# The opening of a DeltaNet and maxout kernel: one root for the inverse squares, a transposition in halves, the fourth query products later, two PSUM tiles exchanged

## The chip, the cores and the metric

The kernel runs on one core of one Trainium2 chip. The metric is the time of one execution in microseconds (us) on the device. Before the change three runs gave 506.69, 509.49 and 509.79 us; the median is 509.49 us. Beside these there is one profiled execution, and all positions and durations below are from it.

## The reference

Two stages follow each other. The first is a recurrence over 768 time steps for 4 batches with 8 heads each, with a state of 48x48 per head. The second is a maxout layer over the 3072 tokens of width 384.

```python
k_n = k / (np.linalg.norm(k, axis=-1, keepdims=True) + 1e-06)
for t in range(S):
    y[:, :, t] = np.einsum('bhd,bhde->bhe', q[:, :, t], state)
    v_old = np.einsum('bhde,bhd->bhe', state, kt)
    state = state + bt[:, :, :, None] * np.einsum('bhd,bhe->bhde', kt, vt - v_old)
...
h = np.maximum(np.maximum(x @ w1, x @ w2), x @ w3)
return h @ w_out
```

## The kernel before

**Tiling.** The recurrence is cut into 12 chunks of 64 steps. Inside a chunk the updates are a unit triangular system; its inverse is built from the Gram matrix of the keys. Two chunks make a group, and there are 6 groups (`GROUPS`). A group's 512 tokens are one tile of the maxout layer. `ffn(m)` is a generator: it issues the matrix products of one tile and yields after each hidden product (`p_h`), and the loop at the end of the kernel puts pieces of the next group's recurrence between the yields. So TensorE (PE) always has the dense products of `ffn` and, between them, the small ones of the recurrence.

**Order.** The whole kernel is issued under a schedule written by hand: each engine executes its instructions in the order in which the program lists them, and waits for others by semaphores. A late instruction therefore holds up everything behind it on its engine.

**The opening.** Before the first `p_h` the first group has to go through the recurrence with little else to do. The stages, with the lines of the profile:

- Keys are loaded, transposed on PE (`turn`, L338; ACT copies the result out, L344), and multiplied to Gram matrices (`gram`, L415). The part for keys gives `at` (L432), the part for queries (index 1) gives `pt` (L426), which is masked later (L399).
- `solve(0)` takes the 32x32 blocks of the first two chunks, with one block per partition, in `x_bl`. The diagonal holds the squares of the key norms. `norm` (L270 to L275) takes the root on ACT and improves it with one Newton step in five small VectorE (DVE) instructions; a reciprocal, a square and a product with beta follow (L532 to L534), and the scaling of `x_bl` (L547). Then 15 steps of two DVE instructions (L561, L565) build `y_bl`, the inverses of the blocks, in halves of 16.
- `y_bl` is transposed back (L573) and `placed` (L505) copies four pieces of it into `ut`, for chunk 0 at once and for chunk 1 over the following stages.
- `halves_t(0)` transposes `ut` (L645, L647) into two tiles `t`. `halves_z` (`p_e`, L685), `halves_u` (`p_f`, L696), `turn_t1` (L630, L632), `join_z` (`p_z`, L713) and `join_u` (`p_j`, L726) join the halves to 32 and then to 64: two products each, copied or negated out of PSUM by ACT (L688, L700, L717, L728) and, for a part, by DVE.
- `scale` (L296, on GpSimd, here POOL) multiplies the values by the key norms, `new` (`p_u`, L771) applies the inverse, `to_y` (`p_y`, L813) multiplies by the masked `pt`, `to_x` (`p_x`, L832) transposes the result into `xt` (L839), and the first `p_h` (L1224) can start. `solve(1)` then runs on DVE between the pieces of `ffn(0)`; its `y_p` lies in PSUM.

**The weights.** They arrive as 64-bit floats, read as pairs of 32-bit words. `weights()` is a generator (`conv`): each call lets ACT convert one piece (L247 to L249) and then finishes the piece *before* it by a shift on DVE (L259) and an addition on POOL (L263, in `joined`). The pieces come in the order of use: piece 0 is for the first `p_h`, piece 1 for the second, and so on. Four calls are made before `ffn(0)`; in the loop the call of step `i` finishes piece `i`+3 (`CONVERTED`). The tile `w_bits` has five buffers and `mant` two, so a later conversion also delays the fetch into its buffer.

**The tables.** `FIRST` says what the loop of `ffn(0)` issues behind the hidden product number `i`+1: `e1` is `halves_z(1)`, `f1` `halves_u(1)`, `k1` and `q1` the products with the state (`p_k`, `p_q`, L743), `z1`, `j1`, `u1`, `y1`, `s1`, `x1` the other stages of chunk 1, `M2` the mask of `pts[2]`, `T4` the transposition of query unit 4, `P4` the query part of Gram unit 4, and `S1` one step of `solve(1)`.

**The end.** The last group uses products of 7 instead of 8 blocks. `crossed_hidden` makes the hidden values in 6 units of 8 small products each (L1163); `bank(n)` gives the PSUM tile of product `n`. Tiles of `ps_ffn` (two buffers) serve products 6 and 7, tiles of `banks` (six buffers) the others. Products 3 and 4 are copied out by ACT (L1193, L1197), 6 and 7 are added by DVE (L1169). `outputs` (L985) then takes its two PSUM tiles from `ps_ffn`.

Of the kernel before, what the change touches and what calls it, by code (L numbers as in the profile page):

```python
# [14 lines left out]
ALU = mybir.AluOpType  # L15
# [8 lines left out]
def kernel(  # L24
# [243 lines left out]
    def norm(out, ksum, root, t):  # L268
# [8 lines left out]
        )  # L277

    def small(name, *shape):
        one = name[-1] == "0" or name[-2:] == "bl" or name == "warm"  # L280
        return work.tile([128, *shape], FP32, name=name, bufs=2 - one)
# [215 lines left out]

    def placed(cc, i, copy=nc.vector.tensor_copy, xs_of=slice(0, 2 * H)):
# [6 lines left out]
        copy(to[:, xs_of], of[:, xs_of])  # L505

    def solve(m):
# [13 lines left out]
        bl = small("bl", BL)  # L521
        norm(bl, diagonal(x), small("root_bl", BL), small("nt_bl", BL))
        if m == 1:
            y = ps_two("y_p").rearrange("p b (j i) -> p (b j) i", i=BL)
            nc.scalar.copy(y, zero.to_broadcast(y.shape))
        if m:
            norms_of(m, bl)
            nc.vector.reciprocal(bl, bl)
        else:
            bl_0.append(bl)  # L530
            bl = small("inv_bl", BL)
            nc.vector.reciprocal(bl, bl_0[0])  # L532
        nc.vector.tensor_tensor(out=bl, in0=bl, in1=bl, op=ALU.mult)
        nc.vector.tensor_tensor(out=bl, in0=bl, in1=beta_bl[:, m] if m else beta_0, op=ALU.mult)  # L534
        if m > 2:
# [35 lines left out]
        if m == 0:  # L571
            back = in_rows(xs[0])
            nc.vector.transpose(out=back, in_=y.rearrange("p c i -> p i c"))  # L573
            yield
            for i in range(4):
                if i % 2:
                    n = H * (i == 3)
                    if n:
                        placed(0, i, nc.vector.tensor_copy, slice(0, n))
                    placed(0, i, nc.scalar.copy, slice(n, 2 * H))  # L580
                else:
                    placed(0, i, nc.vector.tensor_copy)
            return
# [54 lines left out]

    def halves_t(c, parts=(0, 1)):
        if c not in fine:  # L640
            fine[c] = [square("t") for g in range(2)]
        src = [ut[c % NU][:, g].rearrange("p h x -> p (h x)") for g in range(2)]
        dst = [t.rearrange("p h x -> p (h x)") for t in fine[c]]
        if 0 in parts:
            nc.vector.transpose(out=dst[0], in_=src[0])  # L645
        for bb in range(2) if 1 in parts else ():
            nc.vector.transpose(out=dst[1][rows(1 - bb)], in_=src[1][rows(bb)])  # L647

# [27 lines left out]
    def halves_z(c):  # L676
        if c > 1:
            halves_t(c)
        at = [ats[2 * c + g] for g in range(2)]
        second = ut[c % NU].rearrange("p g h (f two x) -> p g h f two x", two=2, x=HB)  # L680
        for hs, p_v, copy in heads_of(c, "p_e", BL):
            for i, h in enumerate(hs):
                for bb, g in TILES:
                    r = rows(bb)
                    nc.tensor.matmul(  # L685
                        p_v[rows(bb ^ g), g, i], at[g][r, h], second[r, g, h, :, 1]
                    )
            copy(zs[c % NU][:, :, span(hs)], p_v)  # L688

# [435 lines left out]
    def crossed_hidden(m, hs):  # L1125
# [24 lines left out]
        for unit in range(2 * PAIRS):  # L1150
# [24 lines left out]
            def bank(n):  # L1175
                if n > 5:
                    return ps_ffn([128, TOK], "p_e")[:, 0:256]
                return banks.tile([128, TOK], FP32, name="p_c", tag="one", bufs=6)[
                    :, 0:256
                ]  # L1180
# [151 lines left out]
    load_q(3, (nc.gpsimd, nc.gpsimd))  # L1332
    load_beta()
    keys(6)
    gram(0, (1,), None, later=True)
# [16 lines left out]
    placed(1, 1, nc.gpsimd.tensor_copy)  # L1352
    blocks(1, nc.gpsimd)
    for _ in range(2):
# [4 lines left out]
    masked(pts[0], by_par(pts[0]))  # L1359
    placed(1, 2)  # L1360
    join_u(0)
# [193 lines left out]
```

## Time and profile before

| | us |
|---|---|
| runs | 506.69, 509.49, 509.79; median 509.49 |
| profiled execution | 507.8 |
| its span, first to last instruction | 506.1 |
| PE busy in the span | 484.4 |
| DVE, ACT, POOL busy | 362.5, 168.7, 186.4 |
| start of the first `p_h` | 45.39 |

The chain of waits goes back from the last instruction to what released it, step by step. The windows give each engine's busy time and the granted TensorE clock (PEclk) in a stretch. The timeline lists instructions in order of time: start, duration, engine, line, what is written and read, and in brackets how long the engine had been idle and who ended that.

### The profile page before, as it was taken

What the parts mean: (1) busy time and instruction counts of PE and PEld (TensorE: products, weight loads), DVE (VectorE), ACT (ScalarE), POOL (GpSimd) and SP (SyncE); (2) the same over time, 40 slices, a digit from 0 to 9 for tenths busy, and PEclk for the clock granted to TensorE, in tenths of its full rate; (3) what the DMA queues carried; (4) which work ended last, traced back from release to release, by engine and by line L of the source; (5) the groups of instructions that cost most, each with busy time, mean ns of one, the idle gap of its engine ahead of it and who ended that gap; (6) DMA issues with size and microseconds to landing.
All of it is one profiled execution on the core that took longest, in us unless ns stands there. A gap on an engine that the chain in (4) does not pass through costs nothing.

```text
span 506.1 us, 18677 instructions
## 1 busy us (share of the span) xinstructions
PE 484.4 (96%) x8064; PEld 338.0 (67%) x8064; DVE 362.5 (72%) x835; ACT 168.7 (33%) x320; POOL 186.4 (37%) x311
## 2 busy tenths in 40 slices
PE   7678899999999999999999999999999999999996
PEld 6567688756565555565555565555797457998795
DVE  5888989868996431799562999565998865467843
ACT  4576854884422142210153200252211042113210
POOL 6424582783491925870495870601000020000000
PEclk9855999999999999999999999999999999999999
DMA  8937979783055925443585552834224321330002
GB/s 111 205 53 207 201 177 147 183 220 91 2 141 128 191 57 122 121 118 99 120 157 124 138 139 62 168 56 93 63 61 88 62 66 25 89 80 0 0 17 47
DMA packets 109122, 53.50 MB, mean 106 GB/s; under 512 B 92209, under 2 KB 102865, under 8 KB 109041
## 3 DMA queue, kind: packets, MB, share of 16 engines
q1 hardware_dynamic: 97280, 31.78, 31.2%
q0 software_dynamic: 9216, 19.85, 15.6%
q8 instruction: 63, 1.03, 0.9%
q10 hardware_dynamic: 2544, 0.69, 0.7%
q14 instruction: 19, 0.15, 0.1%
HBM read 39.17 MB, written 13.11 MB: 103 GB/s over the span
## 4 chain that ended last, share of the span: by engine, by line
PE 82%; DVE 6%; DMA 5%; ACT 2%; issue 1%; SPq 1%; POOL 1%; ACTq 0%; DVEq 0%; POOLq 0%
PE p_h L1224 31%; PE p_o L985 13%; PE p_o L1262 12%; PE p_c L1163 4%; PE p_g L415 3%; PE p_u L771 3%; PE p_m L905 2%; PE p_k L743 2%; PE p_y L813 2%; PE p_q L743 2%; PE p_s L794 2%; PE p_j L726 2%; DMA x_bl<-at_d 1%; DMA qall<-in_q_dram 1%; PE p_e L1163 1%
## 5 line engine op out<-in xcount | busy, mean ns | idle before, releaser
L1224 PE MATMUL p_h<-xt,w_sb 128*128 128x512 f32 (+1 forms) x450 | 187.5, 559 | 1.3 <-issue 0.7
L1224 PEld LDWEIGHTS p_h<-xt,w_sb 128*128 128x128 f32 x450 | 82.5, 193 | 70.0 <-issue 62.4
L1238 DVE TENSOR_TENSOR h<-h,p_h 128x512 f32<-128x512 f32 (+1 forms) x42 | 25.4, 606 | 47.2 <-PE p_h L1224 45.7
L565 DVE TENSOR_TENSOR y_bl<-y_bl,tmp 128x31 f32<-128x31 f32 (+20 forms) x139 | 50.3, 362 | 4.8
L561 DVE TENSOR_TENSOR tmp<-x_bl,y_bl 128x31 f32<-128x31 f32 (+20 forms) x139 | 48.7, 350 | 3.9
L1262 PE MATMUL p_o<-wo_sb,h 128*128 128x384 f32 x144 | 48.9, 490 | 0.0
L373 POOL DMA_DIRECT2D turned<-in_q_dram x72 | 39.1, 551 | 4.3 <-POOL turned L368 2.9
L1262 PEld LDWEIGHTS p_o<-wo_sb,h 128*128 128x128 f32 x144 | 26.8, 190 | 17.2
L1234 ACT ACTIVATE h<-p_h 128x512 f32<-128x512 f32 x24 | 14.3, 597 | 69.3 <-PE p_h L1224 69.2
L263 POOL TENSOR_TENSOR w_sb<-mant,up 128x384 int32<-128x384 int32 x18 | 18.8, 1046 | 37.7 <-DVE mant L259 34.7
L415 PEld LDWEIGHTS p_g<-kqt 48*64 48x64 f32 x1216 | 24.9, 143 | 9.3 <-issue 6.7
L415 PE MATMUL p_g<-kqt 48*64 48x64 f32 (+1 forms) x1216 | 28.1, 243 | 0.9 <-ACT kqt L344 0.8
L1268 ACT COPY o_sb<-p_o 128x384 f32<-128x384 f32 x12 | 5.7, 479 | 62.6 <-PE p_o L1262 56.5
L399 DVE TENSOR_TENSOR pt<-p_g,mask 128x512 f32<-128x512 f32 x20 | 13.8, 689 | 16.2 <-PE p_g L415 16.0
L801 DVE TENSOR_TENSOR st<-st,p_s 48x768 f32<-48x768 f32 (+1 forms) x18 | 17.1, 949 | 11.1 <-PE p_s L794 10.8
L598 POOL DMA_DIRECT2D ut<-y_d x4 | 2.6, 651 | 60.4 <-DMA y_d<-y_bl 60.4
L148 POOL DMA_DIRECT2D v_t<-in_v_dram x14 | 11.5, 829 | 36.0 <-PE p_u L771 36.0
L368 POOL MEMSET turned<- 128x96 f32 x18 | 3.3, 191 | 49.6 <-DVE kqt L389 49.6
L771 PEld LDWEIGHTS p_u<-v_t,ut 64*64 64x64 f32 x768 | 13.7, 144 | 7.9 <-issue 5.9
L432 ACT COPY at<-p_g 128x512 f32<-128x512 f32 x22 | 12.7, 583 | 18.6 <-DVE pt L399 16.1
L373 POOL DMA_DIRECT2D turned<-in_k_dram x32 | 17.4, 553 | 1.2 <-POOL turned L368 1.2
L129 POOL DMA_DIRECT2D kpad<-in_k_dram x24 | 16.4, 691 | 3.0 <-PE p_s L794 3.0
(241 smaller groups left out, 909.2 us busy)
## 6 DMA issues: line engine op xcount, KB each, us to landing
w_bits<-in_moe_w_dram SPq DMA_DIRECT2D x9, 384.0 KB, 5.8
w_bits<-in_moe_w_dram POOLq DMA_DIRECT2D x9, 384.0 KB, 6.3
turned<-in_q_dram POOLq DMA_DIRECT2D x72, 48.0 KB, 2.8
out_dram<-o_sb SPq DMA_DIRECT2D x36, 96.0 KB, 2.3
y_x<-y SPq DMA_DIRECT2D x32, 96.0 KB, 2.2
qall<-y_x SPq DMA_DIRECT2D x32, 96.0 KB, 2.6
v_t<-in_v_dram POOLq DMA_DIRECT2D x14, 192.0 KB, 5.0
at_d<-at SPq DMA_DIRECT2D x72, 32.0 KB, 2.5
```

The lines of the kernel that those rows point to most:

```text
L263: nc.gpsimd.tensor_tensor(out=dst.bitcast(I32), in0=mant_v.bitcast(I32), in1=up_v, op=ALU.add)
L373: (queue, nc.gpsimd)[i].dma_start(out=t[p0 : p0 + 32, bb, at : at + NP * 2 * D].rearrange("p (j x) -> p j x", j=NP), in_=(k, q)[i][2 * bb ...
L415: nc.tensor.matmul(p_g[rows(bb ^ (g * i)), par, c0 : c0 + C * (1 + whole)], kq[:, 0], kq if whole else kq[:, i],)
L561: nc.vector.tensor_tensor(out=t_v, in0=row.to_broadcast(t_v.shape), in1=column.to_broadcast(t_v.shape), op=ALU.mult,)
L565: nc.vector.tensor_tensor(out=rest, in0=rest, in1=t_v, op=ALU.subtract)
L743: nc.tensor.matmul(p_b[rows(bb), par, c0 : c0 + D], kqt[g][dims(par), j, bb ^ g, i], st[dims(par), bb ^ g, g, j],)
L771: nc.tensor.matmul(p_v[rows(bb ^ g), g, i], ut[c % NU][rows(bb), g, h], rhs[rows(bb), g, h],)
L985: nc.tensor.matmul(to[:, g], a[j][:, 128 * g : 128 * (g + 1)], b[j], start=(start and g == j == 0), stop=(stop and g == 1 and j == len(a) ...
L1163: nc.tensor.matmul(to, w[stays], moves, start=(n == 0), stop=(n == len(terms) - 1))
L1224: nc.tensor.matmul(p_h, w_sb[i][:, t, f * 128 : (f + 1) * 128], xt[:, t, lo : lo + w], start=(t == 0), stop=(t == KT - 1),)
L1238: nc.vector.tensor_tensor(out=h, in0=h, in1=p_h, op=ALU.max)
L1262: nc.tensor.matmul(p_o, stays, moves, start=(n == 0), stop=(n == len(terms) - 1))
```

## The change

It has six parts. (1) `inverse_squares` makes 1/(norm+eps)² directly: ACT takes the root of 4·eps²·ksum, one DVE instruction adds eps² and ksum, one takes the reciprocal. The norms themselves, still needed for the values, are made by `first_roots`: a root on ACT and four small instructions on POOL, behind the issue of the beta loads. (2) The solution is transposed by columns in two halves (`turn_back`), the second half first, and `placed` copies by column halves, first the columns that `p_e` reads. (3) The tiles `t` are no longer transposed from `ut`: POOL sets them to zero (`zero_halves`), one DVE transposition turns the first half of the solution (`turn_half`), and eight small copies place its blocks, for chunk 0 on DVE and ACT, for chunk 1 on DVE. (4) The query transposition of unit 3 moves behind `to_x(0)`, its products into step 3 of the loop (`P3` in place of `M3`). (5) One call of `conv` before the solution is left out, and step 6 of the loop gets one. The four pieces of `placed(1, ...)`, one of which POOL copied, move to the stages around `to_y(0)` and all go to DVE; `solve(1)` starts behind `to_x(0)` and not ahead of it. ACT alone copies `p_e` out. (6) In `bank`, products 3 and 4 use `ps_ffn`, 6 and 7 use `banks`.

```diff
+    def inverse_squares(out, square_of, ksum):
+        nc.scalar.activation(out=square_of, in_=ksum, func=Sqrt, scale=4.0 * EPS * EPS)
...
+    def first_roots():
...
+        nc.scalar.sqrt(out, square_of)
+        mult(out=t, in0=out, in1=out, op=ALU.mult)
+        mult(out=t, in0=t, in1=inverse, op=ALU.mult)
+        nc.gpsimd.tensor_scalar(
+            out=t, in0=t, scalar1=-0.5, scalar2=1.5, op0=ALU.mult, op1=ALU.add
+        )
+        mult(out=out, in0=out, in1=t, op=ALU.mult)
...
+    def turn_back(s):
+        cols = slice(HB * s, HB * (s + 1))
+        nc.vector.transpose(
+            out=in_rows(xs[0])[:, cols], in_=ys[0].rearrange("p c i -> p i c")[:, cols]
+        )
...
+    def turn_half():
+        nc.vector.transpose(
+            out=first_half().rearrange("p c x -> p (c x)"),
+            in_=ys[0][:, 0:HB].rearrange("p c i -> p (c i)"),
+        )
+    def halves_t(c, engines):
+        for n, engine in enumerate(engines):
+            f, bb, g = n // 4, n // 2 % 2, n % 2
...
+            copy(
+                fine[c][g][block(bb ^ g, f), :, BL * f : BL * f + HB],
+                first_half()[block(bb, f), :, x0 : x0 + H].rearrange("p c h -> p h c"),
+            )
...
-                if n > 5:
+                if n in (3, 4):
                     return ps_ffn([128, TOK], "p_e")[:, 0:256]
...
     load_beta()
+    first_roots()
+    zero_halves(0)
+    zero_halves(1)
     keys(6)
...
-    turn(3, (1,))
-    some(conv, 1)
     gram(2, (1,), None, later=True)
-    gram(3, (1,), None, later=True)
-    some(solving, HB + 1)
-    halves_t(0)
+    some(solving, HB)
+    turn_back(1)
+    for i in range(4):
+        placed(0, i, A.copy if i % 2 else V.tensor_copy, high)
+    turn_half()
+    halves_t(0, (V, A, V, A, V, A, V, V))
     halves_z(0)
+    turn_back(0)
+    for i in range(4):
+        placed(0, i, V.tensor_copy, low)
     first_norms()
     some(conv, 1)
-    placed(1, 0)
     scale(0, nrm_0[:, 0])
-    placed(1, 1, nc.gpsimd.tensor_copy)
...
     load_v(1, nc.gpsimd)
+    placed(1, 0)
+    placed(1, 2)
+    to_y(0)
     placed(1, 3)
-    to_y(0)
-    halves_t(1)
+    placed(1, 1)
+    halves_t(1, (V, V, V, V, V, V, V, V))
     solving = solve(1)
+    to_x(0)
+    turn(3, (1,))
     some(solving, 1)
-    to_x(0)
     some(conv, 1)
...
-        3: "j1 S1 q1 M3 S1 S1", 4: "u1 T4", 5: "y1", 6: "s1 T5", 7: "x1 T6",
+        3: "j1 S1 q1 P3 S1 S1", 4: "u1 T4", 5: "y1", 6: "s1 T5", 7: "x1 T6",
...
-    CONVERTED = {*range(6), *range(11, 25)}
+    CONVERTED = {*range(7), *range(11, 25)}
```

More of the change, by code (lines that the diff above doesn't have):

```diff
@@ L277, in norm @@
         )
+    EPS = 1e-6
+    def inverse_squares(out, square_of, ksum):
+        nc.scalar.activation(
+            out=square_of, in_=ksum, func=mybir.ActivationFunctionType.Sqrt,
+            scale=4.0 * EPS * EPS,
+        )
+        nc.vector.scalar_tensor_tensor(
+            out=square_of, in0=square_of, scalar=EPS * EPS, in1=ksum,
+            op0=ALU.add, op1=ALU.add,
+        )
+        nc.vector.reciprocal(out, square_of)
+    def first_roots():
+        out, square_of, inverse = bl_0
+        t, mult = small("root_bl", BL), nc.gpsimd.tensor_tensor
+        nc.scalar.sqrt(out, square_of)
[5 more added lines that the diff above has]
+        mult(out=out, in0=out, in1=t, op=ALU.mult)
     def small(name, *shape):
@@ L495, in blocks, with placed @@
         )
-    def placed(cc, i, copy=nc.vector.tensor_copy, xs_of=slice(0, 2 * H)):
+    ys = []
+    def turn_back(s):
[3 more added lines that the diff above has]
+        )
+    def placed(cc, i, copy=nc.vector.tensor_copy, cols=slice(0, BL)):
         bb, half = divmod(i, 2)
@@ L504, in placed @@
         of = in_rows(xs[0])[r, :, 16 * cc : 16 * (cc + 1)].rearrange("p i x -> p x i")
-        copy(to[:, xs_of], of[:, xs_of])
+        copy(to[:, :, cols], of[:, :, cols])
     def solve(m):
@@ L521, in solve @@
         bl = small("bl", BL)
[L522 to L525, printed above, removed]
         if m:
+            norm(bl, diagonal(x), small("root_bl", BL), small("nt_bl", BL))
+            if m == 1:
+                y = ps_two("y_p").rearrange("p b (j i) -> p (b j) i", i=BL)
+                nc.scalar.copy(y, zero.to_broadcast(y.shape))
             norms_of(m, bl)
             nc.vector.reciprocal(bl, bl)
+            nc.vector.tensor_tensor(out=bl, in0=bl, in1=bl, op=ALU.mult)
         else:
[L530 to L534, printed above, removed]
+            bl_0.extend((bl, small("square_bl", BL), small("inv_bl", BL)))
+            bl = small("nt_bl", BL)
+            inverse_squares(bl_0[2], bl_0[1], diagonal(x))
+        nc.vector.tensor_tensor(
+            out=bl, in0=bl if m else bl_0[2], in1=beta_bl[:, m] if m else beta_0,
+            op=ALU.mult,
+        )
         if m > 2:
@@ L571, in solve @@
         if m == 0:
[L572 to L582, printed above, removed]
+            ys.append(y)
             return
@@ L637, with zero_halves, first_half @@
     fine = {}
[L639 to L647, printed above, removed]
+    def zero_halves(c):
+        fine[c] = [square("t") for g in range(2)]
+        zeros(*fine[c])
+    def first_half():
+        return in_wo(1)[:, 0, 0 : HB * BL].rearrange("p (c x) -> p c x", x=BL)
+    def turn_half():
+        nc.vector.transpose(
+            out=first_half().rearrange("p c x -> p (c x)"),
+            in_=ys[0][:, 0:HB].rearrange("p c i -> p (c i)"),
+        )
+    def halves_t(c, engines):
+        for n, engine in enumerate(engines):
+            f, bb, g = n // 4, n // 2 % 2, n % 2
+            x0 = 16 * c + 8 * g
+            copy = nc.scalar.copy if engine is nc.scalar else engine.tensor_copy
+            copy(
+                fine[c][g][block(bb ^ g, f), :, BL * f : BL * f + HB],
+                first_half()[block(bb, f), :, x0 : x0 + H].rearrange("p c h -> p h c"),
+            )
     def heads_of(c, name, w):
@@ L676, in halves_z @@
     def halves_z(c):
-        if c > 1:
-            halves_t(c)
         at = [ats[2 * c + g] for g in range(2)]
@@ L687, in halves_z @@
                     )
-            copy(zs[c % NU][:, :, span(hs)], p_v)
+            nc.scalar.copy(zs[c % NU][:, :, span(hs)], p_v)
     def halves_u(c):
@@ L1340 @@
     gram(1, (1,), None, later=True)
-    turn(3, (1,))
-    some(conv, 1)
     gram(2, (1,), None, later=True)
-    gram(3, (1,), None, later=True)
-    some(solving, HB + 1)
-    halves_t(0)
+    some(solving, HB)
+    low, high = slice(0, HB), slice(HB, BL)
+    turn_back(1)
[3 more added lines that the diff above has]
+    halves_t(0, (V, A, V, A, V, A, V, V))
     halves_z(0)
+    turn_back(0)
+    for i in range(4):
+        placed(0, i, V.tensor_copy, low)
     first_norms()
     some(conv, 1)
-    placed(1, 0)
     scale(0, nrm_0[:, 0])
-    placed(1, 1, nc.gpsimd.tensor_copy)
     blocks(1, nc.gpsimd)
@@ L1359 @@
     masked(pts[0], by_par(pts[0]))
-    placed(1, 2)
     join_u(0)
```

## The prediction

> **What bounds the kernel now.** I read the page's shares and slices first:
>
> ```profile
> PE 484.4 (96%) x8064; PEld 338.0 (67%) x8064; DVE 362.5 (72%) x835; ACT 168.7 (33%) x320; POOL 186.4 (37%) x311
> PEclk9855999999999999999999999999999999999999
> ```
>
> TensorE (PE) is busy throughout, and its granted clock is low only near the start. The windows (stretch, length, busy time of PE, PEld, DVE, ACT, POOL, PEclk) say where PE has slack:
>
> ```profile
> 31.50:34.90 3.40, 3.36 (x122) 3.22 (x118) 2.61 (x6) 2.49 (x7) 0.65 (x1) 0.50 0.22 35
> 38.30:41.70 3.40, 3.15 (x110) 3.17 (x108) 2.82 (x7) 2.48 (x7) 1.86 (x3) 0.50 0.66 210
> 45.10:48.50 3.40, 3.11 (x22) 2.09 (x26) 2.95 (x13) 1.83 (x5) 0.41 (x1) 0.54 0.90 218
> 48.50:62.20 13.70, 11.69 (x464) 9.77 (x458) 12.88 (x31) 9.88 (x21) 6.92 (x7) 0.99 0.96 212
> 62.20:65.60 3.40, 3.40 (x54) 2.39 (x57) 2.90 (x8) 2.07 (x4) 1.00 (x1) 0.55 0.53 137
> 69.00:100.00 31.00, 31.00 (x571) 26.36 (x572) 28.27 (x63) 19.68 (x37) 17.01 (x20) 1.00 0.92 182
> ```
>
> From 62.2 us on PE has no idle time worth naming up to the last tile. So the end is set by the time at which PE's unbroken queue begins; I measure that at the seventh `p_h`, which starts at 68.98. Whatever makes that one earlier makes the end earlier by as much. Then the chain of waits through the opening:
>
> ```profile
> 28.56 0.91 ACT pt L426 x2
> 29.49 1.05 ACT ut L505
> 30.56 0.64 ACT ut L505
> 31.24 1.07 PE p_e L685 x29
> ...
> 45.39 2.93 PE p_h L1224 x6
> ```
>
> After the solution (its last step ends at 26.77) ACT is late with its copies, and `p_e` starts only at 31.24.
>
> **The change, part by part.** All sums are against the profiled execution (507.8 us, span 506.1), which lies 1.7 us under the median of the runs shown (509.49).
>
> *Norms.* From the root (14.71) to the first step (18.13) are 3.42 us. The new chain: root 0.26, one three-operand DVE instruction (no row at this size; at 128x256 L1171 takes 0.43 as a plain addition does, so 0.20, as the 128x32 products), reciprocal 0.35, product with beta 0.19 behind a 0.21 gap, scaling 0.69, gaps 0.22: 2.12. Gain 1.30.
>
> *Roots on POOL.* `first_roots` stands behind the beta loads, which end at 21.6 and 1.3 earlier now: in the middle of the solution. There both operands of a step lie in SBUF, and the timeline at a later, equal place shows what POOL does to that:
>
> ```profile
> 119.62 1.03 POOL L263 TENSOR_TENSOR wo_sb<-mant,up 128x384 int32<-128x384 int32 x1 [0.36 <-DVE tmp L561]
> 119.83 0.90 DVE L561 TENSOR_TENSOR tmp<-x_bl,y_bl 128x60 f32<-128x60 f32 x1
> 120.76 0.22 DVE L565 TENSOR_TENSOR y_bl<-y_bl,tmp 128x60 f32<-128x60 f32 x1
> ```
>
> A step of 0.22 takes 0.90, until POOL is done. Four POOL instructions of 32 elements: at least nothing (POOL's 128x32 copy L538 ended 0.10 after the DVE instruction that held it up), at most 0.35 each (the line through L263, 0.99 at 384, and L296, 1.47 at 768, gives 0.55, less the 0.2 by which the step above is not lengthened). I take 0.17 each, 0.7 in all; ends 0 and 1.4. POOL's zeroing of `t` costs nothing: steps beside MEMSETs (212.5, 152.5 us) keep their length, and POOL idles until 34.25. The solution ends 1.30-0.7 = 0.6 earlier, at 26.2.
>
> *To `p_e`.* Half of the 1.98 transposition is 1.0; ACT's two copies of 256 elements 0.63 each (row at 30.56), waits 0.2: 2.45, so 28.65, 2.6 earlier than 31.24. ACT's delay by `conv` and `pt` is gone.
>
> *To `p_u`.* ACT gets more: three copies into `t` (0.42 each by the line through 0.63 and 1.05; bounds 0.27 and 0.63), then both copies of `p_e` (0.37 each) before `conv` (1.56) and the negations. `p_z` starts at 33.6, 1.7 earlier, `p_u` at 36.9, 1.7 earlier than 38.56. DVE's half transposition, four low copies and `nrm` end at 33.1, in time for its negations.
>
> *To the first `p_h`.* Behind the copy of `u` DVE now has the shift (L259), `placed(1,0)`, `placed(1,2)` and only then the copy of `y`. The shift releases POOL's addition (1.0), and two rows show it and a `placed` copy excluding each other: L263 beside L505 lasted 1.23 and 1.32, each ending 0.87 after the copy. The second copy, coming behind POOL, waits: between 0 and 0.9 late, I take 0.7. [...] So `y` ends at 42.5 where it ended at 43.16, and `p_x` starts at 42.65 (43.30). Of the gain 0.65 is left. The fourth transposition follows: 1.09 at half clock (row at 25.37), 0.57 of it beside ACT's `xt` copies; +0.55. First `p_h` at 45.25 instead of 45.39.
>
> *One piece of weights later.* This is where it turns:
>
> ```profile
> 49.74 0.35 DVE L259 TENSOR_SCALAR mant<-mant 128x384 uint32<-128x384 uint32 x1
> 50.24 0.99 POOL L263 TENSOR_TENSOR w_sb<-mant,up 128x384 int32<-128x384 int32 x1 [4.73 <-DVE mant L259]
> 50.26 1.56 PE L1224 MATMUL p_h<-xt,w_sb 128*128 128x256 f32 x6
> ```
>
> The POOL row finishes piece 2, and the PE row, the second `p_h`, needs piece 1: a whole call of slack. With one call fewer the same place finishes piece 1. It comes behind `solve(1)`'s scaling, and that behind two more copies (1.2) and eight copies of 128 elements (2.3 by the rows 0.37 at 256 and 0.59 at 512; bounds 1.4 and 3.0) in place of three transpositions (2.15); ACT's root, now behind `xt` and the fourth `kqt` copy, is ready at about the same time. So 51.24-0.65+1.35 = 51.95: the second `p_h` starts at 52.0, 1.75 late, though PE is there at 50.2. `p_k` and the DVE subtraction behind it are late by the same, and piece 3 hangs on that: its shift has the place of 56.56, POOL ends at 58.06+1.75, so the fourth `p_h` starts at 59.85 (56.79). The fifth follows `p_j`, `p_q` and the moved `p_g` (0.69) at 64.1 (61.77); the two gaps of PE at 54.7 and 59.2, "issue" in the waits (0.7 and 1.3), I count as covered by the new waits. At full clock the seventh `p_h` would start at 70.45, +1.5; with a half-clock stretch like that of before (62.2 to 65.6), which costs 1.3, +2.8; with two, +4.1.
>
> *Behind the wait.* SP's fetch of piece 8 (46.81) needs the buffer of piece 3, converted only near 53; behind it stand loads of `q` (47.47) and of `v_t` (57.04). The earliest user, `p_t` at 65.95, has some 6 us of cover, `scale` at 72.14 about 5.
>
> *The end.* PE waits for DVE's addition out of the tile of product 6:
>
> ```profile
> 480.05 1.24 PE L985 MATMUL p_o<-wo_sb,h 128*128 128x192 f32 x6 [1.14 <-DVE y_bl L1169]
> ```
>
> With the exchange that tile is that of product 3, copied out at 476.73. The hidden values that this `p_o` reads are done at 476.45, and the sums DVE owes later (483.26) stand ahead of 485.4, when PE comes to them. Gain 1.1; bounds 0 and 1.14.
>
> *Sum.* +2.8-1.1 = +1.7: 507.8 becomes 509.5, on the median 509.49+1.7 = 511.2.
>
> **The clock.** Trace first: PE was 3.36 us busy in 3.40 and kept half clock; full clock came after a stretch with `p_h`. [...]
>
> **Rivals.**
>
> *The opening gets through (faster).* POOL's roots cost nothing (0.7), the copies do not exclude each other (0.7), small copies take 0.18: `y` ends 2.0 earlier, the second `p_h` starts at 49.75, the fifth at 61.85 (now bound by PE's own queue), the seventh at 68.2, -0.8 without a half stretch; with the end -1.9: 507.6. For it speaks the large gain at `p_e`; against it L263's rows. It decides at the second `p_h`: before or after 50.3.
>
> *The clock stays low (slower).* Waits of 1.8 and 2.0 us at the second and fourth `p_h` thin PE's work between 48.5 and 62.2, and from 62.2 only `p_q` and `p_g` follow before the fifth. If no stretch up to 65.6 has enough `p_h`, half clock lasts until 69.0: another 1.3, 512.5; if it starts a stretch earlier too, 513.8. It decides by whether the fifth `p_h` begins after 63.5.
>
> *The end gives nothing.* If DVE's last sums bind instead, +1.1: 512.3.
>
> **Numbers.** Forecast 0.45 (510.2 to 512.3), faster 0.27, clock 0.18, end 0.05, something unseen 0.05. The range takes the faster case less 1.2 for runs of one kernel (they spread by 3.1), and the clock case at its upper price: 506.4 to 514.0. A measurement here tells about 1% (5.1 us) from no change: under 504.4 nothing in these terms leads (0.04), over 514.6 only a clock that stays low for several stretches (0.08), else within.
>
> **What would show it.** Right: `p_e` near 28.7, DVE steps lengthened between 20 and 22, the second and fourth `p_h` released by POOL, no gap before the last tile's first `p_o`. Wrong: no POOL wait at the second `p_h`, or `y` copied before 41.8; or a low clock at other places, which would move the sum by 1.3 a stretch.

## The result, and the profile after

Beside each other the changed kernel took 511.18 us (median of 16 runs, 509.38 to 515.74) and the kernel before 509.05 (16 runs, 506.31 to 511.36). The ratio is 1.0048, with a 95% interval of 1.0025 to 1.007: slower by about half a per cent. The profiled execution has a span of 507.8 us (506.1 before). The page's shares and its slices of the clock:

```profile
PE 485.7 (96%) x8064; PEld 340.0 (67%) x8064; DVE 362.5 (71%) x842; ACT 169.5 (33%) x324; POOL 188.8 (37%) x318
PEclk9657699999999999999999999999999999999999
```

PE is as full as before; what differs lies in the opening. The chain of waits after the changed opening (start, duration, engine, tile, line):

```profile
27.34 1.95 PE p_e L725 x60
...
37.88 0.56 DVE u L816
38.44 0.27 DVE mant L259
38.71 0.52 DVE ut L540
39.24 1.30 DVE ut L540
40.57 0.56 DVE y L857
41.16 0.80 DVE ut L540
...
48.42 1.12 DVE wo_sb L585
49.54 0.28 DVE mant L259
49.97 1.00 POOL w_sb L263
51.01 2.93 PE p_h L1264 x6
...
60.77 1.00 POOL w_sb L263
61.81 1.56 PE p_h L1264 x6
```

`p_e` starts at 27.34 instead of 31.24, almost four microseconds earlier. Yet from 37.88 to 49.97 the chain has DVE alone: copies, the second solution's norms, its scaling (L585), and only then the shift (L259) for piece 1, which POOL finishes at 50.96. The second `p_h` stands at 51.01, later than before (50.26), after 3.01 us in which PE had nothing to do. The fourth waits once more for POOL. The windows (stretch, length, busy time of PE, PEld, DVE, ACT, POOL, PEclk, DMA) show what that does to the clock:

```profile
36.00:39.40 3.40, 3.40 (x128) 3.40 (x123) 2.24 (x6) 2.38 (x6) 2.50 (x4) 0.50 0.62 192
39.40:42.80 3.40, 1.52 (x18) 1.19 (x14) 3.31 (x4) 0.91 (x3) 3.07 (x4) 1.00 0.86 266
42.80:46.20 3.40, 3.30 (x26) 2.31 (x26) 3.07 (x13) 3.38 (x7) 0.00 (x0) 0.50 0.80 166
46.20:49.60 3.40, 1.80 (x120) 1.68 (x116) 3.09 (x11) 0.59 (x2) 0.00 (x0) 1.00 0.02 5
49.60:53.00 3.40, 1.99 (x5) 1.63 (x6) 3.30 (x7) 1.56 (x3) 3.02 (x3) 0.50 0.18 36
53.00:56.40 3.40, 3.40 (x99) 2.75 (x100) 0.82 (x2) 0.52 (x2) 1.90 (x3) 0.50 0.85 235
56.40:59.80 3.40, 3.40 (x50) 2.82 (x45) 2.00 (x6) 2.53 (x6) 0.00 (x0) 0.50 0.94 190
```

From 49.6 to 59.8 there are three stretches at half clock: the first follows a stretch in which PE was busy 1.80 of 3.40, the second one with 1.99. Before, the clock was full from 48.2 to 61.9 and one half stretch followed.

| start of | before | forecast | after |
|---|---|---|---|
| `p_e` | 31.24 | 28.65 | 27.34 |
| `p_u` | 38.56 | 36.9 | 35.73 |
| end of the copy of `y` | 43.16 | 42.5 | 41.13 |
| first `p_h` | 45.39 | 45.25 | 42.90 |
| second `p_h` | 50.26 | 52.0 | 51.01 |
| fourth `p_h` | 56.79 | 59.85 | 61.81 |
| fifth `p_h` | 61.77 | 64.1 | 65.97 |
| seventh `p_h` | 68.98 | 71.8 | 72.92 |

(The seventh stands here as in the chain of waits; the timeline, from which the experiments below are read, has it 0.07 earlier in both.)

From the seventh `p_h` to the end the 3.9 us shrink to 1.7. About 1.2 goes at one place. Before, `p_z` of the second solution waited there for a transfer; now, with PE four microseconds late, it does not. The timeline of PE, of before and then of after:

```profile
102.56 0.90 PE L713 MATMUL p_z<-ut,at 32*32 32x32 f32 x64
103.87 0.25 PE L713 MATMUL p_z<-ut,at 32*32 32x32 f32 x4 [0.41 <-DMA ut<-y_d]
104.40 0.72 PE L713 MATMUL p_z<-ut,at 32*32 32x32 f32 x60 [0.28 <-DMA ut<-y_d]
105.05 2.84 PE L1224 MATMUL p_h<-xt,w_sb 128*128 128x512 f32 x6
```

```profile
106.54 1.35 PE L753 MATMUL p_z<-ut,at 32*32 32x32 f32 x128
107.81 2.84 PE L1264 MATMUL p_h<-xt,w_sb 128*128 128x512 f32 x6
```

The next `p_h` follows 2.49 us after the start of `p_z` before, and 1.27 after. Waits on the way cost the changed kernel 0.7 more: 0.45 at 124.1 and 0.75 at 133.4, against 0.51 at 129.9 before. At the end the wait of 1.14 is gone, as the timeline of PE in the changed kernel shows:

```profile
481.03 1.03 PE L1203 MATMUL p_c<-xt,w_sb 128*128 128x256 f32 x4
481.89 1.14 PE L1025 MATMUL p_o<-wo_sb,h 128*128 128x192 f32 x6
```

3.9 - 1.2 + 0.7 - 1.1 leaves 2.3; the last 0.6 down to 1.7 I did not locate.

### The profile page after: what moved, and what is told of

It is laid out like the page before. It is cut to its first block, busy times and chain, and to the rows that moved or that the text cites. A ratio compares the mean times of both kernels' runs of the same rounds, so it can differ in the third digit from the quotient of the medians.

```text
span 507.8 us, 18690 instructions
## 1 busy us (share of the span) xinstructions
PE 485.7 (96%) x8064; PEld 340.0 (67%) x8064; DVE 362.5 (71%) x842; ACT 169.5 (33%) x324; POOL 188.8 (37%) x318
## 3 DMA queue, kind: packets, MB, share of 16 engines
q8 instruction: 63, 1.03, 0.9%
## 4 chain that ended last, share of the span: by engine, by line
PE 83%; DVE 7%; DMA 3%; ACT 2%; POOL 2%; issue 1%; SPq 1%; DVEq 0%; ACTq 0%; POOLq 0%
PE p_h L1264 30%; PE p_o L1025 13%; PE p_o L1302 12%; PE p_c L1203 5%; PE p_g L441 4%; PE p_u L811 3%; PE p_m L945 2%; PE p_k L783 2%; PE p_y L853 2%; PE p_q L783 2%; PE p_t L364 2%; PE p_s L834 2%; PE p_j L766 1%; PE p_z L753 1%; SPq L129 1%
## 5 line engine op out<-in xcount | busy, mean ns | idle before, releaser
L599 DVE TENSOR_TENSOR tmp<-x_bl,y_bl 128x31 f32<-128x31 f32 (+20 forms) x139 | 50.6, 364 | 3.9
L603 DVE TENSOR_TENSOR y_bl<-y_bl,tmp 128x31 f32<-128x31 f32 (+20 forms) x139 | 48.6, 349 | 4.8
L263 POOL TENSOR_TENSOR w_sb<-mant,up 128x384 int32<-128x384 int32 x18 | 18.5, 1029 | 30.2 <-DVE mant L259 27.4
L1308 ACT COPY o_sb<-p_o 128x384 f32<-128x384 f32 x12 | 5.8, 479 | 62.6 <-PE p_o L1302 56.5
L841 DVE TENSOR_TENSOR st<-st,p_s 48x768 f32<-48x768 f32 (+1 forms) x18 | 17.1, 949 | 10.8 <-PE p_s L834 10.5
L148 POOL DMA_DIRECT2D v_t<-in_v_dram x14 | 11.6, 832 | 34.3 <-PE p_u L811 34.3
L795 DVE TENSOR_TENSOR v_t<-v_t,p_k 128x768 f32<-128x768 f32 x11 | 10.4, 950 | 11.0 <-PE p_k L783 11.0
L399 POOL DMA_DIRECT2D turned<-in_k_dram x32 | 17.5, 556 | 1.2 <-POOL turned L394 1.2
```

What stands on the lines that cost most here:

```text
L263: nc.gpsimd.tensor_tensor(out=dst.bitcast(I32), in0=mant_v.bitcast(I32), in1=up_v, op=ALU.add)
L399: (queue, nc.gpsimd)[i].dma_start(out=t[p0 : p0 + 32, bb, at : at + NP * 2 * D].rearrange("p (j x) -> p j x", j=NP), in_=(k, q)[i][2 * bb ...
L599: nc.vector.tensor_tensor(out=t_v, in0=row.to_broadcast(t_v.shape), in1=column.to_broadcast(t_v.shape), op=ALU.mult,)
L603: nc.vector.tensor_tensor(out=rest, in0=rest, in1=t_v, op=ALU.subtract)
```

## The experiments

Each kernel was timed against the kernel before on the same chip, in 6 or 12 executions; ratios are to the kernel before, with 95% intervals.

**The exchange of the PSUM tiles alone** (kernel before).

```diff
-                if n > 5:
+                if n in (3, 4):
                     return ps_ffn([128, TOK], "p_e")[:, 0:256]
```

> The kernel before, with the exchange of the two PSUM tiles alone. Theory: the whole of the 1.14 us that PE waited ahead of the last tile's first p_o goes, and nothing else moves: span 505.0 (506.1 - 1.1), time 0.998 of the kernel before, first p_o with no idle time above 0.1. Rival (the end gives nothing, DVE's last sums bind instead): the wait stands again further on among the p_o, and the time is 1.000.

Measured: 0.9973 (0.9948 to 0.9997), span 504.9. The timeline of PE at the last tile:

```profile
478.19 1.03 PE L1163 MATMUL p_c<-xt,w_sb 128*128 128x256 f32 x4
479.05 1.14 PE L985 MATMUL p_o<-wo_sb,h 128*128 128x192 f32 x6
```

There is no idle time ahead of `p_o`, and none among the `p_o` behind it, so the rival falls. The 1.14 us of the wait are 0.22%, which the interval holds. The span says less than it seems to: up to the last tile this kernel has the instructions of before, and still its first `p_h` starts at 44.46 (45.39), its clock is half from 29.4 to 53.3 (20.9 to 48.2), and its `p_z` runs at 103.67 in one piece of 1.35, without the wait. So positions move by a microsecond from one execution of the same opening to the next.

**The left-out call of the conversion put back** (changed kernel).

```diff
     turn(2, (1,))
     gram(1, (1,), None, later=True)
+    some(conv, 1)
...
-    CONVERTED = {*range(7), *range(11, 25)}
+    CONVERTED = {*range(6), *range(11, 25)}
```

> The changed kernel, with the call of the weights' conversion that it left out put back in its old place (after the third query transposition) and one call fewer later on. Theory (one piece of weights later is what costs): the second p_h no longer waits for POOL; ACT's three extra instructions (1.56) push p_e back by about 0.8, so the first p_h starts at 43.7 to 44.4 (42.90 in the changed kernel), the second at 49 to 50 (51.01), the seventh at 69 to 70.5 (72.85). Of the gain of 2.4 to 3.9 some 1.2 is given back where p_z waits for the second solution's transfers (the wait that the kernel before has near 104 and the changed one lacks): 1.3 to 2.7 in the end, that is 0.9995 to 1.002 of the kernel before, against 1.0048 for the changed kernel. Rival (the clock or the opening itself sets the seventh p_h, the join is only the last of several things that come at the same time): the seventh p_h stays within 0.8 of 72.85 and the time at 1.004 or above.

Measured: 0.9982 (0.9947 to 1.0017). First `p_h` at 44.22, second at 48.58 and not released by POOL, seventh at 70.02, and PE stands 1.23 us at `p_z` (105.65; the row names an ACT instruction, not the transfer): near what the theory had, the second `p_h` and the time a little ahead of it. The interval lies below that of the changed kernel, whose loss goes with this one call.

**The same call left out of the kernel before, alone.**

```diff
     turn(3, (1,))
-    some(conv, 1)
     gram(2, (1,), None, later=True)
...
-    CONVERTED = {*range(6), *range(11, 25)}
+    CONVERTED = {*range(7), *range(11, 25)}
```

> The kernel before with the early call of the weights' conversion left out and one more later on: the change's one piece later, alone. ACT's 1.56 ahead of the copies of the solution go, so p_e starts 0.7 earlier (30.5 where it was 31.24). Theory (the call costs only because DVE's queue is longer at the same time, by two placed copies and the norms' place): by itself it makes the second p_h start at 50.5 to 51 behind POOL (50.26), the third and fourth 0.4 to 1.3 later: time 1.001 to 1.003. Rival (the call by itself costs what undoing it in the changed kernel gave, 0.66%): second p_h at 51.5 or later, seventh 2 us or more later, time 1.005 or above. Rival (no cost): the gain at p_e comes through, time 0.999 or below.

Measured: 1.0044 (1.0018 to 1.007). The call costs by itself, and more than I thought; the interval holds the upper end of the theory and the rival's 1.005, so their difference stays open. The place is not the second `p_h` (50.95, without a wait, as half clock lasted until 53.6 in this profile) but the fourth, whose piece 3 comes from POOL:

```profile
59.07 0.98 POOL L263 TENSOR_TENSOR w_sb<-mant,up 128x384 int32<-128x384 int32 x1 [4.04 <-DVE mant L259]
...
60.11 1.33 PE L1224 MATMUL p_h<-xt,w_sb 128*128 128x256 f32 x3 [2.10 <-POOL w_sb L263]
```

**Piece 1 joined earlier, with the same number of calls** (changed kernel).

```diff
     to_y(0)
+    some(conv, 1)
     placed(1, 3)
...
     some(solving, 1)
-    some(conv, 1)
```

> The changed kernel, with the third call of the weights' conversion (it joins piece 1) moved from behind the second solution's scaling to right behind the copies of y. ACT has 2.65 us free there. Theory: piece 1 is ready near 43.5, the second p_h starts when PE comes to it, near 48.1 (51.01), not released by POOL; the third waits for piece 2 instead, near 54.6 (57.47), the fourth near 59 (61.81), the seventh near 70 (72.85). The second solution ends about 1 us later by the shift and by POOL's addition beside the copies, and of the 2.8 us some 1.2 to 2 goes into the wait of p_z near 104: 0.8 to 1.6 left, time 1.0015 to 1.003. Rival (the clock): with the wait gone the stretch from 49.6 to 59.9 runs at full clock, the seventh p_h starts before 69 and the time is 1.000 or less. Rival (no effect): the wait only moves to the third p_h, the seventh stays at 72.85 and the time at 1.005.

Measured: 1.0021 (0.9987 to 1.0054). The second `p_h` starts at 49.13 without POOL, the third at 55.82 after 1.09 us for POOL, the seventh at 71.83. A wait came up that I had not expected: `p_k` stands 1.83 us for DVE's addition to the state (L841), which is queued behind the second solution's norms and scaling. So the weights were only the first of two things behind them. By time the kernel is told apart neither from the kernel before nor from the changed one.

**The fourth query products back in their old place** (changed kernel).

```diff
+    turn(3, (1,))
     gram(2, (1,), None, later=True)
+    gram(3, (1,), None, later=True)
     some(solving, HB)
...
     to_x(0)
-    turn(3, (1,))
...
-        3: "j1 S1 q1 P3 S1 S1",
+        3: "j1 S1 q1 M3 S1 S1",
```

> The changed kernel, with the fourth transposition and the fourth query products back ahead of the solution's end, where they were before. Theory: p_e starts 1 to 1.6 later than 27.34, as PE and ACT have the fourth products first; the first p_h within 0.6 of 42.90, since it gets back the transposition (about 0.5); the second p_h, which waits for POOL, within 0.6 of 51.01; the fifth 0.7 earlier without the products ahead of it: time 1.003 to 1.005 of the kernel before, so the move of these products is worth little either way. Rival (the moved products are what makes the stretch after the first p_h thin or late): the seventh p_h comes more than 1.5 earlier and the time falls to 1.001 or less. Rival (the move was worth much): the first p_h starts after 44 and the time is above 1.006.

Measured: 1.0069 (1.0039 to 1.01). `p_e` at 30.43 (27.34) and the first `p_h` at 46.19 (42.90): here the second rival was right, the move is worth 3 us at the first `p_h`. In its old place the fourth transposition stands 3.33 us, up to 25.43, for a transfer of queries, and `p_e` comes behind it; the changed kernel has nothing there that needs this transfer. At the second (53.70, behind a wait of 1.01 for POOL) it is 2.7. By time the two kernels are not told apart, since the intervals overlap.

**The copies of `y` ahead of the placed copies** (changed kernel).

```diff
+    to_y(0)
     placed(1, 0)
     placed(1, 2)
-    to_y(0)
     placed(1, 3)
```

> The changed kernel, with the copies of y ahead of the two placed copies on DVE, so that a placed copy is no longer between the weights' addition on POOL and the copy of y. Theory: the copy of y reads PSUM and is not held by POOL, it follows p_y at 39.6 and p_x starts near 40.25 (41.27), the first p_h near 41.9 (42.90); one placed copy is still doubled beside POOL. The second p_h still waits for POOL, as the placed copies stand ahead of the shift as before: 51.0, and the time is that of the changed kernel, 1.004 to 1.006. Rival (the start of p_x sets the end): all later p_h come 1.0 earlier, time 1.003 or less. Rival (the copy of y is held by POOL as well): it ends at 40.6 or later and p_x gains less than 0.5.

Measured: 1.0092 (1.0063 to 1.0121). The timeline of PE:

```profile
40.36 0.93 PE L872 MATMUL p_x<-ident,y 128*128 128x128 f32 x6 [0.78 <-DVE y L857]
...
41.98 1.53 PE L1264 MATMUL p_h<-xt,w_sb 128*128 128x256 f32 x6 [0.26 <-ACT xt L879]
...
51.93 2.93 PE L1264 MATMUL p_h<-xt,w_sb 128*128 128x256 f32 x6 [6.03 <-POOL w_sb L263]
```

`p_x` and the first `p_h` come 0.9 earlier, as expected (a copy out of PSUM kept its length beside POOL in the kernel before as well: that of `y` at 42.60 took 0.56 beside L263, which ran from 41.82 to 43.14, and that of `u` at 40.81, with POOL idle, 0.56), and the second `p_h` does not come earlier at all: it waits 6 us. What PE gains ahead of DVE's queue is lost in it. By the ratios the kernel is 0.4% slower still than the changed one (the intervals overlap a little), and I have no explanation for that; the profile has half clock at 66.5 to 70.0 and at 110.9 to 117.7, and 1.71 of waiting for a transfer at 110.9.

**PE's waits filled with spare products** (changed kernel; they go to a PSUM tile that nobody reads).

```diff
+    busy(5, ident)
     halves_z(0)
...
+    busy(5, ident)
     join_z(0)
...
+    busy(6, ident)
     to_x(0)
...
+        if i in (0, 2):
+            busy(20 - 7 * i, ident)
```

> The changed kernel, with spare products of 128x128 by 128 columns (they go into a PSUM tile that nobody reads) put into PE's waits: 5 ahead of p_e, 5 ahead of p_z, 6 ahead of p_x, 20 ahead of the second p_h, 6 ahead of the fourth. They fill waits of 1.35, 1.46, 1.72, 3.01 and 0.88 us, and POOL, DVE and ACT get not one instruction more. Theory (the granted clock follows how full PE was a few us earlier, and the waits bring it down): no half-clock stretch after 46, the second p_h takes 1.5 where it took 2.9, p_f and p_k half of theirs, the seventh p_h starts at 69 to 70.5 (72.85); 1 to 2.5 is left in the end, time 1.000 to 1.003 of the kernel before. Rival (the stretches come from something other than PE's waits): half clock again between 46 and 62 over two stretches or more, seventh p_h not before 72, time 1.004 or above. Third way (clock up, but POOL's and DVE's chain to the fourth p_h is what binds): half clock gone, fourth p_h within 0.6 of 61.81, time 1.003 to 1.005.

Measured: 1.0102 (1.0078 to 1.0126). The windows, and PE's timeline at 65.7:

```profile
47.80:51.70 3.90, 3.84 (x35) 3.75 (x34) 3.60 (x11) 0.42 (x1) 1.44 (x2) 1.00 0.02 4
51.70:55.10 3.40, 3.40 (x136) 2.92 (x134) 2.32 (x3) 1.93 (x6) 3.01 (x4) 1.00 0.51 142
55.10:58.50 3.40, 3.40 (x88) 2.92 (x81) 3.03 (x10) 3.32 (x7) 0.57 (x2) 1.00 1.03 260
...
61.90:65.10 3.20, 0.86 (x60) 0.74 (x52) 0.92 (x4) 3.16 (x6) 0.99 (x1) 1.00 1.16 207
65.10:71.90 6.80, 6.20 (x104) 5.01 (x105) 4.41 (x11) 0.32 (x2) 2.01 (x3) 0.50 0.52 104
```

```profile
65.70 1.14 PE L441 MATMUL p_g<-kqt 48*64 48x64 f32 x32 [2.94 <-ACT up L249]
```

With PE full, the clock stays full where the changed kernel had three half stretches, and the third `p_h` starts at 55.10 (57.47), the fourth at 59.44 (61.81). That is one profile; beside the rows of the last section, and since the spare products are its one difference from the changed kernel (PE busy 3.84 of 3.90 from 47.8, where that one had 1.80 of 3.40 from 46.2), it says that the waits brought the clock down here. Then PE stands 2.94 us ahead of `p_g`, in which it is busy 0.86 of 3.20, and two half stretches follow. The ACT row named there ended at 65.18, half a microsecond too early to be the releaser with certainty; see the last section. The seventh `p_h` starts at 74.64, where 69 to 70.5 was expected, and the time lies above every range given. In time the filler costs; where the rest of the 1% goes I did not locate.

**The second solution's write ahead of the transfers of `at`** (kernel before).

```diff
-            some(solving, (3, 2, 2, 2, 3, 3, 3, 3, 2, 2)[i - 4])
+            some(solving, (3, 2, 2, 2, 3, 3, 3, 4, 2, 1)[i - 4])
```

> The kernel before, with the write of the second solution (two transfers on SP) issued ahead of the four transfers of at that SP holds it behind; nothing else moves. Theory: p_z near 104 waits in the kernel before for the chain solution, write, reading back, so the write 3.7 earlier takes that wait away: 1.2 us from one p_h to the next there (8.73 us from the 19th full-width row of p_h at 99.78 to the next at 108.51, to 7.5), time 0.9975. It is this wait that the changed kernel, being late, does not have, and so its loss at the seventh p_h shrinks from 3.9 to 2.8. Rival (the wait's cause is the reading back, or the queue behind it): the write comes earlier and p_z waits the same, time 1.000.

Measured: 1.0012 (0.999 to 1.0034): no gain. `p_z` does run without a break in the profile,

```profile
108.05 1.35 PE L713 MATMUL p_z<-ut,at 32*32 32x32 f32 x128
```

but PE comes there at 108.05, 5.5 us later than before, since PE stood 5.11 us for a transfer of queries at 28.7; that PE had no wait proves nothing about the write. The exchange's profile has the write in its old place and no wait either, with PE there at 103.67 instead of 102.56: whether the wait is paid hangs on when PE comes. By the times the earlier write gains nothing like 1.2 us, and that figure is an account of two profiles, not of the two medians.

**Three edits together** (changed kernel: one more call behind the copies of `y`, these ahead of the placed copies, the write earlier).

```diff
-    placed(1, 0)
-    placed(1, 2)
     to_y(0)
+    some(conv, 1)
+    placed(1, 0)
+    placed(1, 2)
...
-    CONVERTED = {*range(7), *range(11, 25)}
+    CONVERTED = {*range(6), *range(11, 25)}
...
+            some(solving, (3, 2, 2, 2, 3, 3, 3, 4, 2, 1)[i - 4])
```

> The changed kernel with three edits: one more call of the weights' conversion behind the copies of y, where ACT is free, and one fewer later on (pieces 1, 2 and 3 are joined a call earlier); the copies of y ahead of the placed copies; the second solution's write ahead of the transfers of at. Theory: no p_h waits for POOL, the first starts near 42.5, the second near 47.5, the seventh at 67 to 69 with the clock as it falls, no wait at p_z near 101, none at the last tile: against the kernel before 1 to 2 earlier at the seventh p_h, 1.2 at p_z and 1.1 at the end, time 0.991 to 0.994. Rival (the stage from 48 to 62 is bound by the recurrence through DVE and ACT, not by PE's start): the seventh p_h not before 69.5, time 0.9955 to 0.998, which is what the exchange of the tiles and the earlier write give alone.

Measured: 1.0011 (0.9996 to 1.0027), worse than either side had it. The second `p_h` starts at 47.13 and waits for nothing; then the timeline shows

```profile
50.48 1.22 DVE L585 TENSOR_TENSOR wo_sb<-wo_sb,bl 128x1024 f32<-128x1024 f32 x1
51.62 0.35 DVE L259 TENSOR_SCALAR mant<-mant 128x384 uint32<-128x384 uint32 x1
51.88 0.95 DVE L841 TENSOR_TENSOR st<-st,p_s 128x768 f32<-128x768 f32 x1
...
52.98 0.50 PE L736 MATMUL p_f<-z,t 64*64 64x32 f32 x9 [4.29 <-DVE tmp L599]
```

`p_f` waits 4.29 us and starts 0.15 after L841 ends (52.83): L841 is what empties the PSUM tile of `p_s`, and with `y_p` holding one of three such tiles, `p_f` has to have it (I read this from the pool of three; the trace names a DVE instruction of the same moment). The wait of the second `p_h` has become a wait of `p_f`, behind the same DVE queue.

**DVE's queue in another order** (changed kernel: the call ahead of the second solution's norms, its scaling behind the addition to the state).

```diff
+        if m == 1:
+            yield
         nc.vector.tensor_tensor(out=xb, in0=xb, in1=by, op=ALU.mult)
...
-    some(solving, 1)
     some(conv, 1)
+    some(solving, 1)
...
-        0: "e1 s0 S1 S1",
+        0: "e1 s0 S1 S1 S1",
```

> The changed kernel, with two things on DVE's queue between 45 and 51 put in another order: the call that joins piece 1 ahead of the second solution's norms, and the scaling of the second solution (1.22) behind the addition to the state. No instruction is added or taken away. Theory (from the runs so far: DVE, busy without a break from the copies of u at 38 to the state's addition at 50.7, is what the stage waits for, and every gain of PE ahead of it is lost there): the shift of piece 1 at 45.1, POOL done at 46.5, the state's addition ends at 49.9 (50.67), the second p_h starts at 48.1 behind p_s with no wait for POOL (51.01), p_f right behind it, the third p_h near 54.6 (57.47, it then waits for piece 2), the seventh near 70 (72.85); time 0.9985 to 1.003 of the kernel before against 1.0048. Rival (PE's half clock is what makes the stage long, DVE's order only shifts the waits): seventh p_h not before 72 and time above 1.0035. Rival (the second solution, later by 1.2, is waited for further on): seventh p_h near 70, but the wait of p_z near 104 comes back with 1 us or more and the time is 1.003 or above.

Measured: 1.0012 (0.9982 to 1.0042), in the range expected, though its interval touches that of the changed kernel. Its profile is of the longest of its executions and is read for one thing only. The second `p_h` does not wait for POOL (51.06, right behind `p_s`), but the norms, now beside POOL, are held. DVE, then POOL:

```profile
49.25 0.71 DVE L273 TENSOR_TENSOR nt_bl<-nt_bl,wo_sb 128x32 f32<-128x32 f32 x1
49.99 2.17 DVE L274 TENSOR_TENSOR nt_bl<-nt_bl,root_bl 128x32 f32<-128x32 f32 x1
```

```profile
48.89 0.99 POOL L263 TENSOR_TENSOR w_sb<-mant,up 128x384 int32<-128x384 int32 x1 [3.15 <-DVE nt_bl L271]
49.84 0.76 POOL L224 DMA_DIRECT2D w_bits<-in_moe_w_dram  x1
50.61 1.50 POOL L322 TENSOR_TENSOR v_t<-v_t,nrm 128x768 f32<-128x768 f32 x1
```

An instruction of 0.19 takes 2.17 and ends 0.05 after POOL's last. In this execution the state's addition ends at 55.3 and `p_k` waits for it; what the order cost or gave in the shorter ones, no profile shows.

**The shorter norm chain alone** (kernel before, with `inverse_squares` and `first_roots`).

```diff
+            inverse_squares(bl_0[2], bl_0[1], diagonal(x))
...
     load_beta()
+    first_roots()
     keys(6)
```

> The kernel before, with the shorter norm chain and the roots on POOL alone: solution, copies, query products, conversion calls and PSUM tiles as they were. Theory: the chain from root to first step takes 2.0 us where it took 3.4, POOL's four small instructions cost the solution less than 0.1, and as DVE's and PE's work behind it keeps its order, all of it comes 1.3 to 1.4 earlier: p_e at 29.9 (31.24), first p_h at 44.0 (45.39), second at 48.9 (50.26), seventh at 67.6 (68.98) with the clock as before; the end earlier by as much, less the p_z wait near 104 (up to 1.2 of it): time 0.997 to 0.9995. Rival (the gain is worth nothing, since the transfers or the weights' pieces set the first p_h): first p_h within 0.4 of 45.39, time 1.000. Rival (POOL's roots hold the solution's steps up): steps between 20 and 23 lengthened to 0.4 and more, the solution's end earlier by less than 0.7.

Measured: 0.9982 (0.9957 to 1.0007); the expected 0.997 to 0.9995 lies around it, and no gain is just inside the interval. DVE's timeline:

```profile
14.65 0.21 DVE L287 SCALAR_TENSOR_TENSOR square_bl<-square_bl,x_bl 128x32 f32<-128x32 f32 x1 [0.32 <-ACT square_bl L283]
...
16.35 0.19 DVE L590 TENSOR_TENSOR tmp<-x_bl,y_bl 128x30 f32<-128x30 f32 x1
```

With the root at 14.37 the chain takes 1.98. The first `p_h` starts at 42.55 and the seventh at 66.06, more than 1.4 earlier; but this profile has no half clock from 39.9 to 500, and the rest is not shown to be the edit's.

**Norm chain and exchange together** (kernel before; both diffs above).

> The kernel before with two parts of the change alone: the shorter norm chain with the roots on POOL, and the exchange of the two PSUM tiles. Theory: the two gains stand at the two ends of the kernel and share nothing, so their ratios multiply: 0.9973 x 0.9982 = 0.9955, that is 2.3 us under the kernel before; no wait at the last tile's first p_o. Rival (the opening's gain does not reach the end, b_norm's 0.9982 was chance): time 0.997 to 0.998, that of the exchange alone.

Measured: 0.9972 (0.9942 to 1.0001), median 507.55. That is the ratio of the exchange alone: the sum is neither shown nor excluded. Of all kernels here this one and the exchange alone have the lowest ratios; their intervals overlap those of the norm chain alone and of the changed kernel with its call put back. All four lie below the changed kernel, with intervals that do not meet its own.

## Why the forecast held

**The total.** 511.2 was forecast, 511.18 measured. That they meet to the hundredth is luck: the forecast was +1.7 on 509.49, and beside a kernel before of 509.05 the change measured +2.1. The working behind it was right in its turning point and wrong in terms that nearly cancel in the profiles. Of its own four signs of being right two came (POOL releases the second and the fourth `p_h`; no gap at the last tile) and two did not (`p_e` at 27.34, not 28.7; no DVE step there above 0.32, where 0.28 is usual). Of its three signs of being wrong two came: `y` was copied by 41.13, before 41.8, and the clock was low at other places.

**Right.** The norm chain: 1.43 gained (1.30). The placed copy that comes second to POOL: 1.30 instead of 0.60, late by the 0.7 that I took between 0 and 0.9. The weights one piece late: the second and the fourth `p_h` are released by POOL, and putting the call back brought the ratio from 1.0048 to 0.9982, while leaving it out of the kernel before alone cost 0.44%. The end: 1.14 gone.

**Mis-sized: POOL's roots.** I took 0.7. They cost some 0.05: no step beside them is longer than 0.32, where 0.28 is usual. After's timeline:

```profile
21.25 0.25 POOL L298 TENSOR_TENSOR root_bl<-bl 128x32 f32<-128x32 f32 x1
21.33 0.32 DVE L599 TENSOR_TENSOR tmp<-x_bl,y_bl 128x120 f32<-128x120 f32 x1
21.58 0.25 POOL L299 TENSOR_TENSOR root_bl<-root_bl,inv_bl 128x32 f32<-128x32 f32 x1
21.68 0.29 DVE L603 TENSOR_TENSOR y_bl<-y_bl,tmp 128x120 f32<-128x120 f32 x1
```

The price was drawn from a line through instructions of 384 and 768 elements; at 32 they take 0.21 to 0.25, not 0.55. With the run itself starting 0.65 earlier (the transposition of the blocks at 12.04, 12.69 before) this makes up the 1.3 by which `p_e` and the copy of `y` came sooner than forecast. The first `p_h` gained 1.0 more by the clock: it was full from 39.4 to 42.8, so that `p_x` took 0.93 (1.52 before) and the fourth transposition 0.60, where I had 1.09.

**Mis-sized: the half stretches.** The term "+2.8 with one half-clock stretch" failed: there were three, from 49.6 to 59.9, and the seventh `p_h` came 3.9 late. That it would be one, and not none or two, was my estimate and no run shows it. What came is the course of my rival in which the clock stays low (waits of 1.8 and 2.0 thin PE's work; they were 3.01 and 0.88, and the stretches from 46.2 and 49.6 had PE busy for 1.80 and 1.99), and its condition, a fifth `p_h` after 63.5, was met. But that sign could not decide: the forecast's own fifth stood at 64.1. Nor did I work out the step from the fifth to the seventh: by the rows of before it takes 7.21 with one half stretch in it, which makes 71.3 and not 71.8. At half clock the second `p_h` took 2.93 (1.56 before), the third 2.72 (0.92 and 0.81 in two parts) and `p_f` and `p_k` 1.93 and 1.94 (1.14 and 1.13), and so the fourth came 2.0 after its forecast although the second came 1.0 ahead. In the filler run, without the waits, there is no half clock from 41.2 to 65.1.

**Left out: `p_z` near 104.** I had written that PE has no idle time worth naming from 62.2 on. The wait there took 1.2 from the loss in this pair of profiles. In the medians it does not show (the earlier write gained nothing). What cancels there is not shown; stretches of half clock, of which the first began at 20.9 before and at 15.7 in the exchange with the same opening, would be the simplest.

**Where the opening's gain went.** From the end of the first solution to the end of the state's addition on DVE are 24.6 us before (26.77 to 51.36) and 25.9 after (24.73 to 50.67). The solution ends 2.0 earlier, the state's addition 0.7. In DVE's queue between the copies of `u` and that addition there are four placed copies (3.5 us) where there was one (0.6): the others had lain beside earlier waits, one of them on POOL. The three experiments that took a wait away in this stage without shortening the queue (the earlier join, the copies of `y` first, the three edits) each met the next wait behind it.

## What to carry to other kernels

An earlier start is worth only what is left at the next instruction that another engine waits for; so sum the whole in-order queue up to that instruction, on the engine that holds it, before the gain is booked. A conversion that runs one piece ahead of its user has one piece of slack and no more: leaving out one call cost 0.44% by itself. And take a part that shares nothing with the rest, as the exchange of two tiles did, out of a change and keep it.

## What the runs showed of the hardware

**Where the half stretches lie.** In the profiles of before and of the changed kernel every stretch of full or half clock that lies between 5 and 66 us is a multiple of 3.41 us long, to within 0.02 (13.65, 27.31, 13.65 and 3.41 before; 10.24, 23.89, three of 3.41, and 10.24 in the changed kernel). They begin elsewhere in each profile: the first half stretch at 20.9, 15.5, 15.7, 26.3, 16.8 us in five of them (before, changed, exchange, norm chain, fourth products put back), of which the first and the third have the same opening. Between 40 and 100 us half clock adds up to 11.6 us before, 13.7 after, 0 in the kernel with the norm chain alone and 24.6 in the one with the fourth products put back. So one profile of such an opening is one draw, and effects under a per cent need the medians.

**What stood ahead of half clock.** The stretches between 10 and 125 us are cut into pieces of 3.41 us here. The full-clock pieces that half clock followed had PE busy for 1.30 and 2.09 us before (from 17.5 and 58.5) and for 1.77, 1.54 and 1.80 in the changed kernel (from 12.1, 39.4 and 46.2). The least busy ones that full clock followed had 2.27 before (from 14.1) and 2.32 and 2.53 in the changed kernel (from 66.7 and 59.9). In all fourteen profiles half clock followed 26 of 26 such pieces under 1.8 us, 9 of 15 between 1.8 and 2.2, and 1 of 289 above; the norm chain alone had 1.81 and 1.87 and kept full clock. So no one number parts the two kinds here.

**What stood ahead of full clock.** The prediction put full clock beside a stretch with `p_h`. It came without one too: the stretch 36.0 to 39.4 above has only `p_u` and `p_y`, 3.40 of 3.40 busy, and full clock follows. But 53.0 to 56.4, as busy and with `p_h` in it from 51.01 to 53.94, is followed by half clock. On the pieces above, none of 43 at half clock with PE busy under 2.8 us was followed by full clock (in before and the changed kernel the seven had 1.06 to 2.66), and of 46 with PE busy throughout, 31 were (3 of 5 in these two). What sets these apart stays open.

**Small instructions beside POOL.** Beside a chain of POOL instructions a DVE product of 32 elements took 2.17 us instead of 0.19 and ended 0.05 after POOL's last (DVE's queue in another order), while POOL's own products of 32 elements cost DVE 0.04 at most: in the changed kernel the DVE step at 21.33 overlaps POOL's 0.25 by 0.17 and is longer by 0.04. What sets the two apart was not tried. Placed copies of 0.60 took 0.80 beside POOL's issue of the loads of `v_t` (41.16 and 41.97 in the changed kernel), but one beside its fetch of `w_bits` kept 0.60 (38.57 before).

**Waits named "issue".** PE stands 0.7 to 1.3 us inside runs of small or dense products with no releaser in the trace (0.69 at 55.37 and 1.27 at 60.46 before, 1.10 at 69.47 in the changed kernel; each time is that of the end). A packet of the queue that the page calls an instruction queue (63 packets, 1.03 MB: 16 KB each) begins 2.5 and 2.8 us ahead of these ends before (52.9, 57.7) and 2.5 in the changed kernel (67.0); in the filler run one begins 3.1 ahead of the end of the wait of 2.94 (62.6). Other such packets have no wait behind them (62.4 and 66.3 before). That the waits have to do with the packets is my guess from this nearness and was not tried.
